# A four-stage residual vector quantizer on one core: the order of every engine's queue and the engines of its free steps are replaced

## The chip, the cores and the metric

The kernel runs on one core of one Trainium2 chip. Time is what the device takes for one execution, in microseconds. Beside the time of several runs there is one profiled execution, whose trace gives each instruction's start and end; its span runs from the first to the last instruction. The engines are TensorE (PE, matmuls), VectorE (DVE), ScalarE (ACT), GpSimd (POOL) and SyncE (SP, which here issues the large DMAs). Each engine works its own queue in the order in which the program put it there, and waits at an instruction until its inputs and buffers are ready.

## The reference

For two sequences of 16,000 rows of 512 values the kernel computes a three-tap filter along time, a SiLU, a four-stage residual quantization against codebooks of 8 entries each, and a second three-tap filter over the sum of the chosen entries.

```python
for i in range(K):                       # K = 3
    z = z + xp[:, i:i+T, :] * dw_enc[i][None, None, :]
z = _silu(z)
res = z
for s in range(Nq):                      # Nq = 4
    cb = codebooks[s]                    # 8 x 512
    d2 = (res . res)[..., None] - 2.0 * res . cb + (cb . cb)
    idx = d2.argmin(-1)
    sel = cb[idx]
    q = q + sel
    res = res - sel
for i in range(K):
    y = y + qp[:, i:i+T, :] * dw_dec[i][None, None, :]
```

## The kernel before

The rows are cut into 18 tiles, n = 0 to 17. A tile has G groups of 128 rows; G is 6 and 8 for the first two tiles, 16 for fourteen, 8 and 6 for the last two. The 512 channels lie in four blocks of 128 on the partitions. Each tile goes through these stages, whose names are the keys of the steps in the code (line numbers are those of the profile):

- load: SP issues one transposing DMA for each group (L599, L607, L613) into one of three buffers XT. The first two tiles come by plain DMAs and are turned on PE (pad, L580 and L590).
- taps, in two halves of two channel blocks: three scalings by a filter weight for each block (L640 on ACT, L641 on DVE, into TA and TB) and two additions on DVE (L393).
- exp (L646, ACT), plus1 (L647 on ACT or L648 on DVE), recip (L658, ACT) and gate (L393, DVE, ZB<-ZB,EX): the SiLU. exp and recip need different tables of ACT, so two or three halves go through exp, then the same ones through recip.
- score0: on PE the squared length of each row and its products with all 32 entries (L670, L677); DVE reads them out of PSUM (L711, L712).
- decide: the first three choices, a chain of small DVE operations, with a transpose and a correction on PE in between (L754, L764) and a small copy of the result by ACT or DVE (L758, L759). POOL copies one-hot rows (L746, L749).
- win0: the one-hot rows are turned on PE (L787) and copied (L792). resid: PE subtracts the three chosen entries from z in 4 units of two steps (L835, L840); the result is cast back into ZB by ACT (L862) or DVE (L863). The last two steps of a unit feed two casts.
- score3, decide3: the fourth choice in the same manner (L878, L879). win3: its one-hot rows are turned (L804) and copied (L810).
- back: the decoder filter as a matmul for each pair of groups (L912, L914, L916), cast into one of four buffers YB by ACT (L921) or DVE (L922), and stored by SP (L949).

The program is not written in its final order. The class Plan collects 2,404 steps, each with its engine, a cost for planning, and its dependencies. A step with the engine pair ACT and DVE is a free step: six kinds are free, the scalings of taps, plus1, the copies of pad, win0, win3 and of decide's transposed choice, the casts of resid and of back, and three small scalings of the setup. Two strings settle everything: RANK gives each step a number, and each engine's queue is sorted by it; WHERE gives one letter, A or D, for each free step in the order of the code.

```python
queue[s["on"]].append(s["n"])
for q in queue.values():
    q.sort(key=lambda n: -rank[n])
```

The loop in Plan.order then goes through the queues and hands out PSUM banks; where by its own costs PE would stand idle for over a microsecond it puts dummy matmuls ahead of the step (fill, L969). There are 413 of these in the kernel before. The dependencies, and with them every wait, come from the tiles that a step reads and writes.

Of the kernel before, what the change touches and what calls it, by code (L numbers as in the profile page):

```python
# [185 lines left out]
def kernel(  # L186
# [30 lines left out]
    NA = 4  # L217
    QUOTA = {"ACT": 4, "DVE": 4}
    DIGITS = "0123456789abcdefghijklmnopqrstuvwxyzABCDEFGHIJKLMNOPQRSTUVWXYZ"
    RANK = ("00010300000501090M0f0a0N080K0e010b030f0X0l0e0i0b0U0h0q0s000o000q0A0b0d0n0E040s0708020f0a0e060g0109040607090d0f0i0j02080a"  # L220
            "0c0e0g0h0m05050d070709020406040a0c0608010b0i0r03020A0H0K0v050c0T0V0Y1115191b0q0E0F0c0G0r0j0m0o1e1m1p1d1o1u0h0o0t1j1w1y0p"
            "0d0k0m030i0t0z0F0H0J0L0P0S0g0j0l0p0k0v0D0y0I0B0O0x0l130u0m0u0G0w0C0j1i0p1r0n1l0k1g0Q0h0g0R0W100Z120n1f171614181a1h1c1k0w"
            "0z0y1A0B1E0r0s1M1O1N1P1Q1R1S0k0t0L0u1T1V1X1Z1W1Y202122230l0v250w242628292a2b2c2d0n0x0P0y0z2i2j0A0B0T0R0C0D2n2m0E0F0U0V0G"
            "0H2t2A2D2H2J0K120N170P191m0M141t1s1n1q0x1t1x1v1z0D271B1C1D0C1F1G1H1I0J0O0h050b0708030i0g0a0604090c0f020j0l0d1L0I1J1K1U0M"
            "0N2e0Q2l0S2w0W2v0X2x0I0J2z2B2C2E2G2I2K0o0L130O2M2N2O2R2T2W2X2Y2Z300p0Q330R31343637383a3b3c0q0S3e0T0U3i3j0V0W3l1b0X0Y1d3n"
            "0Z101e3o11123t3w3x3z3B151l1c1t1f1u1p191n1a1o1f2h2k2f2g2o2p2q2r102L0t0o0B0u0k0m0e0q0A0n0z0r0p0v0x0s0y0w0Z2s0Y2u2y2F112P16"
            "182U152V2S3239353d1a3p1c3r1g3F1i3E13143D16173I3L3K3N3P3Q3S0r1d1p1g3U3W3Y403V3Z414243440s1i471j464a4c4b4d4e4f4g0u1k1v1l1m"
            "1x1y1n1o1z1A1p1q1D4u1r1s1C4x1v1w4H1x1z4Q4V4X4Z531L1P1S1Y2024211R1X1W221Y1Q1W1Y201Z1P1V1V2627181b3R1e1h3X48454k4l4p4s0t1t"
            "4z1u4v4w4y4A4C4D4E4F4G4I0v1y4L1A4J4K4M4P4R4S4U4W0w1D1J1F1G541M1I1J1O1N1K1M1S1R1N1O1U1T1T1Z5C21225F5H5J5L5O265W29282b2a2f"
            "2a292e2b2u2q2l2A2r2t2r2n2x2q2p0G0O0Q0E0D0T0M0I0N0C0R0F0K0J0P0H0S0L3k3g3h3f3m1f3q3s1k491h3v3u3y3A1j3C3H1q4m15110Y1a0Z0W17"  # L230
            "100V161912181c14130X0U3M3J3O1m3T1r1s4h1w4o1B4B1E4N1G4Y1B1C511E1H565a585c5e5h2Q5j0y1U5s1X5l5n5p5r5w5y5A5E5G5I0z235M245K5N"
            "5R5Q5T5Y60630C2d652f2g2e2d2h2i6e2f2l2m2i2h2n2o2j2k2t2v6C2u2z6L6N6P6T702I732S2G327D2K2L2C2M2E2C2N2D2R2F2F2U2H312O2N4n4i4q"
            "4j4r1F4t4O1K571h1i1b1v1u1s1g1d1r1x1w1o1n1l1e1q1k1j504T1I1H521L55591Q5o5d5f5g5b5i5m5k5q1Z5B215P255Z276425275V282c676b6a6d"
            "6f6h3G6j0D2p6r2s6m6o6q6s6u6v6w6x6y6z0E2w2o2y6A6D6F6E6G6H6I6J0F2B2s2D2F2w2x2G2H2z2v2J2K2A2B2V2Y2K7v33357J38397Q7S7W7Y813g"
            "2W3k303m312W3j2Z3w373b3n323l353d3o8j3q38342j2k6k2C2E6S6W6V7274767a0H2Q7f2T7c7e7g7i7j7k7m7o7q7s0I2Z2J307t7u7y7x7z7A7B7C0J"
            "347F36372P2Q3b3c2U2T3e3f2V2X3h3i2Y893p3r8h3t3v8n8p8r8t8A3G8I413u423w3z3N3l3U3o3r403t3P3v3v3O3m3Q3p3E1C1F1I1E1P1G1A1z1y1O"
            "1M1B1H1N1D1L1K1J5u5v5x5t5z235D5S2c6B625X615U6669686c2g6t1U1X251V1T1R292a1S26222820231Q241W0x0A6l6g6n6i6p2p2m6K2t6X2u752y"
            "772I7H2O2P7d2W2X7n7r7p7w7E7G7I0K3a2R3d7K7M7N7O7V7X7Z8486880L3s343u8b8f8i8l8o8q8s8u0M3x8x3y3z3a3c3C3D3h3d3E3H3i3f3J3K3j3k"
            "3T3V983W3Y9e9j9l9n9q453y4l3L4g3N3M4h3J4p3M3L4d3E4q3Q3Q4s3P4t3S3S6Q6O6M6R6U6Y6Z712M7L2n2d2c2i2e2j2k2l2h2w2m2g2b2q2o2r0B0G"
            "2s787b797h7l2L2N7P2S837R7T807U8285878a338w368y398G3b8H3A3B8F3F3I8K8O8N8Q8S8U8V0N3R8X3S8Y909295919497999a9b0O3X3r3Z9d9f9h"  # L240
            "9g9i9k9m9o0P439r46473z3A484a3C3F4b4c9F3D4e4f3G3H4i4j9R4m4na4a7a9abad4xak4B3U4C3V494A3T4F3X3Y4E3W4Gaz414W484R4c4g3L3M8R44"
            "499y9C9A9E9J9M9O0Q4k9U4o9Q9T9W9Z9Ya3a6aaacae0R4wag4zahajamanaparasau0U4Daw4H4I3Z404J4K41424L4M43464O4PaQ454S4Tb14X4Ybabd"
            "bgbjbn594h5c4k5f4n4E5e4p5n4u4z5g4o5r4A4H5k4r5o4t4B2L2A2I2G2J2E2z2M2y2x2v2D2R2B2Q2P2O2H8d8e8g8c8k8v8m8z3e8M8E8B8C8D8J3g8L"
            "8P3n9c30352Y36372U3a38323c33392S2V312Z2X2T938Z8W8T963s3q9p3x9x3B9H3I9V3Ka14r4uaf4v4yalaqaoataxaBaD0S4NaM4QaGaIaKaNaRaTaU"
            "aVaWaX0T4UaZ4VaYb0b2b3b4b5b6b70W4Z4a5152bi4d55564g4f585a4j4i5b5d4m4l5h5lbK5i5pbNbQbTbVbY5F4G5J4N5P4P4I5I4L5X4U4Q5O4O5S4R"
            "4N5Q4Q5T4T4R9u9s9t9v9w9B9z9D3Oai3l3s3f3h3t3i3g3w3k3u3p3n3o3q3m3e3x3j9L9I9G9K9N9P9S9X3Raya0a5a2a8av3YaAaC44aS47b849bb4bbo"
            "5054bl5357bpbsbrbvbybAbC0V5j4q5mbEbGbIbMbHbLbPbRbWbZ0X5u4x5wc1c3c5c6c7c8c9cb0Z5xcg5y5z4Bck5A5B4E4D5C5D4F4H5G5H4K4J5K5NcD"
            "5M5RcGcKcMcOcV5Zd1634X6f594Z6o5b6q5f506g586n5c516e576j5d525q5sbU5t5vc4cacccdcecfci0Y5E4I5LcmcqcscwcycAcCcEcJcL105WcP5YcN"
            "cRcUcTcWcXcYcZ12614W64654Z5066675251686955546c6d56ds6h6idF6m6pdNdUdWe0e56ye76G5s6S5y536O5v6UeT546M5u6Q5w566F5r6N5t553O3J"
            "3D3N3F3G3H3R3P3U3C3y3B3I3K3A3V3TaEaJaHaFaLaPaOb94ebtbfbebcbhbkbmbqbu4sc03Z4h404f4344424c3W4b4d4e484a4746453XbxbwbBbzbDbJ"  # L250
            "bFbO4vc24zcn4Ccp4McF5U5VcQ6062d3d6d5d9dbdedg136adj6bdidkdmdpdndqdtdvdxdy146kdC6ldzdAdHdGdKdMdPdS166sdV6u6v5h5k6w6x5ie86A"
            "6C5o5n6D6Eel5p6H6Jeu6L6PeFeIeKeMeO6VeW7e5K7m5Q577h5O7n5P587f5L7o5R597c5J7g5N5a4ybXbS4wchclcjco4Sd04o4w4y4x4n4q4r4v4A4u4s"
            "4p4t4l4j4k4m4icvcuctcrcxcBczcH4Ydfd2cS4VcId4d7d8da53dr5adQ5ee25ge66r6tdX6z6Beaefecehekemen176Ieq6KepeteweAevexeBeCeDeE18"
            "6ReG6TeHeJeLeNePeQeReS1b6XeU6Z70f0f67172f25C75765E5G777bfi5I7j7lfB7q7ufQfUfXfYg77Ggd7L5Z7Wgx5d7Kgj7Mgm5b7Q607U645c7S627X"
            "635e6W6YeV7374f3f5f4f7f8f9fb19795H7dfdfgfhfjfkflfmfnfofp1a7i5M7kfqfrfsfvfwfxfyfA1e7pfE7r7tfL5S7w7x5U5T7A7B5W5X7E7Fgc5Y7J"
            "7Ngk7T7ZgygCgGgHgI86gK8ggQ8i6e5h886a8bgN5f8e6c8f6d5g8m6g8n6h5i4K4O4L4J4G4C4D4P4M4FdldcdhdddodudwdB5mejdJdIdEdDdLdRdOdT5q"
            "ey5xeY5zeZ787afeftfufzfCfDe9fF1c7sfK7vfGfHfIfJfMfNfOfPfRfS1d7z5V7CfTfVfWfZg0g2g5g81i7Hgg7P7R61gu8081656682836867848769gL"
            "8h8lgSgTgUgVgW8qgY8v6l8x6m5k8s6j8u6k5j4T4V4S4Y4X4U4W1115e1dZdYe3e45l5jeb5Af1eeeiedegeoeresez5Bfa5Dfc5Fff7y7Dg1g4g3g6g9ga"
            "eXgb1f7Ige7Ogfghgignglgogpgqgrgs1g7Vgw7YgtgvgAgzgBgDgEgF1h85gJ898agM6b8c8dgPgO8j8kgR6f8o8pgX6i8r8tgZh0h1h2h38wh48yh58Ah6"
            "5m8z6n5l")  # L260
    WHERE = ("DADDADAADAADAADAADDDDDDDDDDAADADDAADDAAAAAADDDADDDDDDADDADADDAADADDDDDAADADAAAAADDDDDDDADADDAADADDDDDADAAAAAADADAAAAAAAA"
            "ADDADAAAAAAADAAAAAAAADDDDADDADDDADDDDDAAADDDDAADAAAAADADAAAAAADDDDADDDDAAADDDDDDDDDDAAAAAAAAADAAAAAAADADADAAAAAAADDAAAAA"
            "AAADDDDADDDDDDDDDDDDDAADAADAAAAAAAAAAAAAAAAADDDDDDDDDDDAADDDDDDDDDADAAAADAAADAAAAADAADDDAAAAAADAAAAAAAAAADDDDDDDDDDDADDD"
            "DDDAADDDADAAAAAAAAAAAAAAAADDDDDDDDDDDDDDDDDDADDAADADAAAAAADAAAAAAAAADAAAAAAAADDAAADAAAADDDDDDDDDDDDDDDDDDDDDDDDAAADAADAD"
            "AAAAAAAAADDADDDDDDDDDDDDADDDDDDDDDDAAADADADDDAAAAAADDAAAAADADDAADAAAADDDDDDDDDDDDDDDADADAAAAADDAAAADDDDAADDDDDDDDDDDDADD"
            "DADADDDA")
# [740 lines left out]
```

## Time and profile before

| | before |
|---|---|
| median of 3 runs | 602.56 us (601.38 to 603.75) |
| span of the profiled execution | 600.7 us |
| busy: PE, DVE, ACT, POOL | 500.1, 562.4, 548.7, 53.6 us |
| instructions on DVE and ACT | 1125 and 419 (26 of ACT's are table loads) |

The profiled execution has no time of its own beside its span; the median of the runs stands 1.9 us above that span. In the rows that follow, "busy" is the time in which at least one instruction of the group ran, "mean ns" is the duration of one, and what stands behind the second bar is the idle time of the engine just before instructions of the group and what ended it. A row of a timeline has the start, the duration, the engine, the line, the operation and its tiles.

### The profile page before, as it was taken

The page shows a single profiled execution, that of the slowest core. Times are in us where ns is not written, and L with a number is a line of the kernel's source. Part 1 is how long each engine was busy: PE and PEld are TensorE (multiplying, and loading weights), DVE is VectorE, ACT ScalarE, POOL GpSimd, SP SyncE. Part 2 cuts the span into 40 slices and gives each one's busy share as a digit, 9 for nine tenths or more (in the row PEclk, how much of TensorE's full clock was granted, in tenths as well). Part 3 has the DMA queues.
Part 4 walks back from the last instruction along what each step waited for, and adds up shares of the span by engine and source line. Part 5 has one row for each costly group of instructions (what it writes and reads, how often), then busy time and mean ns, then how long its engine had stood idle before and what let it go on. Part 6 is the DMA issues. An engine that isn't in the chain of part 4 may idle for free.

```text
span 600.7 us, 27780 instructions
## 1 busy us (share of the span) xinstructions
PE 500.1 (83%) x12632; PEld 241.1 (40%) x12632; DVE 562.4 (94%) x1125; ACT 548.7 (91%) x419; POOL 53.6 (9%) x86
## 2 busy tenths in 40 slices
...
DVE  7999999999999999999999999999999999996764
ACT  4889999999999999999999999999999999996454
...
GB/s 222 84 93 73 84 102 90 75 133 124 73 97 139 138 117 107 174 155 92 142 140 95 168 123 188 147 108 115 82 179 88 177 56 109 4 144 142 39 183 183
DMA packets 155564, 71.84 MB, mean 120 GB/s; under 512 B 146895, under 2 KB 146927, under 8 KB 155318
## 3 DMA queue, kind: packets, MB, share of 16 engines
...
## 4 chain that ended last, share of the span: by engine, by line
DVE 23%; PE 12%; SPq 8%; ACT 8%; issue 5%; DMA 1%; DVEq 0%; ACTq 0%
SPq L599 7%; DVE ZB L393 6%; DVE TB L641 3%; PE banks L835 3%; PE banks L912 3%; PE banks L677 2%; PE banks L840 2%; DVE TA L393 2%; ACT ZB L862 2%; DVE TA L641 2%; ACT EX L646 2%; DVE EX L648 1%; ACT YB L921 1%; DVE ZB L863 1%; DMA XT<-in_x_dram 1%
## 5 line engine op out<-in xcount | busy, mean ns | idle before, releaser
L921 ACT CAST YB<-banks 128x1024 bf16<-128x1024 f32 x115 | 111.6, 1037 | 12.9 <-PE banks L912 6.6
L646 ACT ACTIVATE EX<-ZB 128x4096 bf16<-128x4096 bf16 (+2 forms) x36 | 115.3, 3205 | 4.1 <-DVE ZB L393 3.9
L658 ACT ACTIVATE EX<-EX 128x4096 bf16<-128x4096 bf16 (+2 forms) x36 | 115.1, 3201 | 0.1
L862 ACT CAST ZB<-banks 128x1024 bf16<-128x1024 f32 (+2 forms) x109 | 97.7, 952 | 16.3 <-PE banks L840 16.3
L969 PE MATMUL banks<-MSK,IDENT 128*128 128x512 bf16 x413 | 103.5, 392 | 6.4 <-issue 2.6
L677 PE MATMUL banks<-ZB 128*32 128x64 bf16 x8064 | 90.4, 197 | 9.7 <-issue 6.0
L677 PEld LDWEIGHTS <-ZB 128*32 128x32 bf16 x8064 | 75.6, 95 | 52.6 <-issue 44.7
L912 PE MATMUL banks<-WDEC,OHW 128*128 128x512 bf16 x252 | 74.0, 382 | 14.3 <-ACT ZB L862 8.0
L840 PE MATMUL banks<-OHR,WR 32*128 32x512 bf16 (+2 forms) x1152 | 81.6, 355 | 0.1
L641 DVE TENSOR_SCALAR TB<-XT,WENC 128x2048 bf16<-128x2048 bf16 (+2 forms) x115 | 76.7, 676 | 1.6 <-issue 1.2
L393 DVE TENSOR_TENSOR ZB<-TA,TB 128x4096 bf16<-128x4096 bf16 (+2 forms) x36 | 73.0, 2028 | 0.8 <-ACT TB L640 0.4
L393 DVE TENSOR_TENSOR TA<-TA,TB 128x4096 bf16<-128x4096 bf16 (+2 forms) x36 | 72.7, 2020 | 0.5
L393 DVE TENSOR_TENSOR ZB<-ZB,EX 128x4096 bf16<-128x4096 bf16 (+2 forms) x36 | 72.3, 2017 | 0.3 <-ACT EX L658 0.2
L835 PE MATMUL banks<-ZB,IDENT 64*64 64x512 bf16 (+2 forms) x576 | 54.3, 368 | 13.4 <-DVE ZB L863 3.0
L749 POOL COPY OHD<-OHA 128x256 bf16<-128x256 bf16 (+2 forms) x36 | 27.5, 764 | 417.3 <-DVE OHA L393 417.3
L969 PEld LDWEIGHTS <-IDENT 128*128 128x128 bf16 x413 | 38.4, 100 | 49.7 <-issue 13.8
L640 ACT ACTIVATE TB<-XT,WENC 128x2048 bf16<-128x2048 bf16 (+2 forms) x29 | 53.2, 1845 | 3.6 <-DVE TA L393 2.0
L835 PE MATMUL banks<-ZB,UP 64*64 64x512 bf16 (+2 forms) x576 | 52.4, 353 | 0.0
L840 PEld LDWEIGHTS <-WR 32*128 32x128 bf16 x1152 | 23.4, 92 | 58.3 <-issue 50.1
L641 DVE TENSOR_SCALAR TA<-XT,WENC 128x2048 bf16<-128x2048 bf16 (+2 forms) x66 | 44.0, 676 | 1.5 <-DMA XT<-in_x_dram 1.4
L835 PE MATMUL banks<-ZB,DOWN 64*64 64x512 bf16 (+2 forms) x576 | 41.4, 363 | 0.0
L863 DVE CAST ZB<-banks 128x1024 bf16<-128x1024 f32 (+2 forms) x35 | 32.8, 950 | 7.3 <-PE banks L840 7.3
...
## 6 DMA issues: line engine op xcount, KB each, us to landing
...
out_dram<-YB SPq DMA_DIRECT2D x31, 2.0 KB
...
```

Source lines behind the costliest of these rows:

```text
L393: add("DVE", cost, key, lambda: nc.vector.tensor_tensor(out=out, in0=a, in1=b, op=op), reads, writes, **kw)
L640: either({"ACT": act(R), "DVE": dve(R, 3.84) + 0.06}, key, lambda dst=dst, src=src, w=w: nc.scalar.mul(dst, src, w), lambda dst=dst, src=s ...
L641: lambda dst=dst, src=src, w=w: nc.vector.tensor_scalar(out=dst, in0=src, scalar1=w, scalar2=None, op0=ALU.mult),
L646: add("ACT", act(2 * R), ("exp", n, h), lambda: nc.scalar.activation(v(ex), Z, ACT.Exp, scale=-1.0), zt, [("EX", sl), "ACTTAB"], hold="E")
L658: nc.scalar.add_instruction(mybir.InstActivation(name=nc.get_next_instruction_name(), engine=mybir.EngineType.Activation, func=ACT.Reciprocal,
L677: nc.tensor.matmul(o[HB * q:HB * (q + 1), u * ZW:(u + 1) * ZW].rearrange("p (s c) -> p s c", s=2), lhsT=blk, rhs=both, start=False, stop=( ...
L835: nc.tensor.matmul(at(r)[to], lhsT=dia[h, h], rhs=Z[h, i, r:G:RG, :], start=start, stop=False)
L840: nc.tensor.matmul(at(r), lhsT=WR[v][g, i * P:(i + 1) * P], rhs=W[g, v // 3, 0:rows_of[r], :], start=False, stop=stop)
L862: either({"ACT": act_psum(2 * k * P), "DVE": dve(2 * k * P)}, key(1), lambda dst=dst, src=src: nc.scalar.copy(dst, src()), lambda dst=dst, ...
L912: nc.tensor.matmul(o, lhsT=W[:, k, PADC:PADC + P], rhs=WDEC[u], start=True, stop=not wrap)
L921: either({"ACT": act_psum(1024), "DVE": dve(1024)}, key, lambda dst=dst, box=box: nc.scalar.copy(dst, ps(box)), lambda dst=dst, box=box: n ...
L969: nc.tensor.matmul(PS[j // 2][:, 512 * (j % 2):512 * (j % 2) + NMK * ZW], lhsT=IDENT, rhs=MSK.rearrange("p u w -> p (u w)"), start=True, s ...
```

## The change

Only the two strings are replaced, RANK (4,808 characters, two for each step) and WHERE. Every step and its function stay.

```diff
-    RANK = ("00010300000501090M0f0a0N080K0e010b030f0X0l0e0i0b0U0h0q0s000o000q0A0b0d0n0E040s0708020f0a0e060g0109040607090d0f0i0j02080a"
+    RANK = ("00010200000a0905090b070G060F0c010408080f0h0a0g0g100d0i0m000v080g0E00020c260n2D0k1J04270p0z014h0703010306070c0g0h0j02050b"
...
-    WHERE = ("DADDADAADAADAADAADDDDDDDDDDAADADDAADDAAAAAADDDADDDDDDADDADADDAADADDDDDAADADAAAAADDDDDDDADADDAADADDDDDADAAAAAADADAAAAAAAA"
+    WHERE = ("AADDAAAADAAAAADDADDDDDDDDDDDADADDAAAAADAAAADDDDDDADAAADDADADADDDDDDDAAADAAAAAAAADDDDDDDDAADDAADDADDDDAAADAAADADAAAAAAAAA"
...
```

What it makes of the queues, read from the built programs. Free steps that change their engine, as net counts (a 2048 is a tile 128x2048, and so on):

| | DVE | ACT |
|---|---|---|
| taps, 2048 into TB (L641, L640) | 88 to 99 | 24 to 13 |
| taps, 2048 into TA | 51 to 49 | 5 to 7 |
| taps, 1024 into TA; 768 into TA; 768 into TB | 8 to 7; 7 to 6; 13 to 15 | 0 to 1; 1 to 2; 3 to 1 |
| resid casts, 1024 (L863, L862) | 19 to 13 | 93 to 99 |
| resid casts, 512; 256 | 13 to 8; 3 to 4 | 11 to 16; 5 to 4 |
| win3 copies, 1024; 384 (L810) | 9 to 5; 1 to 0 | 5 to 9; 1 to 2 |
| pad copies, 1024 (L590) | 5 to 3 | 2 to 4 |
| back casts (L922, L921) | 11 to 10 | 115 to 116 |
| win0 copies, 1024 (L792) | 9 to 10 | 5 to 4 |
| plus1, 2048; 1536 (L648, L647) | 3 to 2; 3 to 4 | 1 to 2; 1 to 0 |
| setup scaling WR | 1 to 0 | 2 to 3 |
| all instructions but table loads | 1125 to 1116 | 393 to 402 |

ACT still changes its table 26 times, in the same groups of two and three halves. The dummy matmuls go from 413 to 423; ahead of the first score0 there are 20 instead of 39, and a new group of 3 stands before the last step of PE.

The order near the end, for tiles 14 to 17. In PE's queue, a number behind a star is a count of steps:

```diff
-resid14*4 score015*2 resid14*3 score016 decide15 score016 resid14 back13 decide15 back13*4 decide15 score314 decide15 score314 back13*3 win015 score314 resid15 decide16 resid15 score314 decide16 resid15*2 score017 decide16 resid15*2 decide16 score017 resid15*2 win314 win016
+resid14*4 score015*2 resid14*3 score016 resid14 decide15 back13 decide15 score016 back13*3 score314 decide15 back13 decide15 back13 score314 back13 win015 score314 back13 resid15*2 decide16 score314 resid15 decide16 resid15*3 decide16 resid15 score017 decide16 score017 resid15 win016 win314
```

On DVE the two gates of tile 17 were instructions 999 and 1003 of 1125, ahead of most of decide15; they become 1041 and 1042 of 1116, behind decide15, most of decide16 and the first cast of resid15. On ACT the two recips of tile 17 were 347 and 349 of 393 and become 364 and 367 of 402, behind six and seven casts of back13. In SP's queue loads and stores of the same tiles are interleaved otherwise: from tile 9 on, the longest run of loads between two stores was 18 (the last of load14 and all 17 of load15, ahead of the first store of tile 9) and is 16 (load12, ahead of the first store of tile 6). In the setup some steps of tables that are not needed at once move behind the first taps, gates and decide steps.

More of the change, by code (lines that the diff above doesn't have):

```diff
@@ L219 @@
     DIGITS = "0123456789abcdefghijklmnopqrstuvwxyzABCDEFGHIJKLMNOPQRSTUVWXYZ"
-    RANK = ("00010300000501090M0f0a0N080K0e010b030f0X0l0e0i0b0U0h0q0s000o000q0A0b0d0n0E040s0708020f0a0e060g0109040607090d0f0i0j02080a"
[L221 to L260, printed above, removed]
```

50 lines of the change are left out of this document (45 added, 5 removed).

## The prediction

> **What bounds the kernel now.** I read the page's sums and slices first, then the busy time of each engine by stretches of the span.
>
> ```profile
> PE 500.1 (83%) x12632; PEld 241.1 (40%) x12632; DVE 562.4 (94%) x1125; ACT 548.7 (91%) x419; POOL 53.6 (9%) x86
> DVE  7999999999999999999999999999999999996764
> ACT  4889999999999999999999999999999999996454
> ```
>
> ```profile
> core 0: us, PE busy (x) PEld busy (x) DVE busy (x) ACT busy (x) POOL busy (x), PEclk, DMA share, GB/s
> 0.00:60.00 60.00, 44.04 (x549) 22.55 (x549) 53.91 (x153) 47.06 (x61) 4.77 (x29) 0.91 0.51 118
> 60.00:523.91 463.91, 386.29 (x10146) 184.76 (x10142) 456.17 (x827) 453.22 (x306) 45.36 (x47) 0.99 0.61 117
> 523.91:537.75 13.84, 13.46 (x415) 5.78 (x407) 12.86 (x26) 13.68 (x12) 0.97 (x1) 1.00 0.45 155
> 537.75:552.71 14.96, 14.53 (x390) 7.20 (x382) 11.38 (x43) 9.69 (x11) 1.14 (x4) 1.00 0.31 109
> 552.71:594.55 41.84, 41.78 (x1157) 20.85 (x1153) 26.76 (x79) 24.41 (x31) 1.37 (x6) 1.00 0.37 128
> 594.55:600.70 6.15, 0.00 (x1) 0.00 (x0) 1.33 (x2) 0.66 (x1) 0.00 (x0) 0.77 0.62 202
> ```
>
> From 60 to 524 us DVE is busy for 456.17 of 463.91 us and ACT for 453.22: two engines at 98%, and neither can give the other work without becoming the bound. From 524 to 594.55 DVE and ACT thin out and PE is full (13.46 + 14.53 + 41.78 of 70.64 us). So there are two regimes. The front runs at the pace of DVE and ACT together; the tail, from the first resid step of tile 14 on, is PE's remaining queue without a hole, then the last casts and stores. Its landmarks:
>
> ```profile
> 523.23 0.68 DVE L792 COPY OHR<-banks 128x1024 bf16<-128x1024 bf16 x1
> 523.71 0.41 PE L835 MATMUL banks<-ZB,IDENT 64*64 64x512 bf16 x4
> 536.80 0.95 DVE L393 TENSOR_TENSOR ZB<-ZB,EX 128x1536 bf16<-128x1536 bf16 x1
> 552.71 0.34 PE L670 MATMUL banks<-MSK,IDENT 128*128 128x384 bf16 x1
> 593.96 0.59 PE L912 MATMUL banks<-WDEC,OHW 128*128 128x512 bf16 x2
> ```
>
> The first row is win0 of tile 14, the second the start of its resid, the third the last gate (tile 17), the fourth the start of score0 of tile 17, the fifth PE's last matmuls. The last gate is ready at 537.75 and PE takes it up only at 552.71: 15 us of slack. What shortens the kernel is an earlier arrival at resid14, as long as that slack isn't used up.
>
> **What the moved steps cost.** The dependent work stays; the free steps change sides. Prices, from the groups with shapes kept apart:
>
> ```profile
> L641 DVE TENSOR_SCALAR TB<-XT,WENC 128x2048 bf16<-128x2048 bf16 x88 | 65.1, 747 | 1.5 <-issue 1.2
> L641 DVE TENSOR_SCALAR TA<-XT,WENC 128x2048 bf16<-128x2048 bf16 x51 | 37.5, 744 | 1.5 <-DMA XT<-in_x_dram 1.4
> L863 DVE CAST ZB<-banks 128x1024 bf16<-128x1024 f32 x19 | 23.1, 1216 | 2.6 <-PE banks L840 2.6
> L863 DVE CAST ZB<-banks 128x512 bf16<-128x512 f32 x13 | 8.7, 684 | 4.5 <-PE banks L840 4.5
> L810 DVE COPY OHW<-banks 128x1024 bf16<-128x1024 bf16 x9 | 6.1, 680 | 0.1
> L922 DVE CAST YB<-banks 128x1024 bf16<-128x1024 f32 x11 | 13.3, 1219 | 2.0 <-PE banks L912 1.7 <-PE banks L914 0.3
> ```
>
> ```profile
> L640 ACT ACTIVATE TB<-XT,WENC 128x2048 bf16<-128x2048 bf16 x24 | 48.0, 2014 | 3.4 <-DVE TA L393 2.0 <-DMA XT<-in_x_dram 1.4
> L640 ACT ACTIVATE TA<-XT,WENC 128x2048 bf16<-128x2048 bf16 x5 | 10.0, 2003 | 0.3 <-DVE OHA L741 0.3
> L862 ACT CAST ZB<-banks 128x1024 bf16<-128x1024 f32 x93 | 89.9, 1027 | 12.4 <-PE banks L840 12.4
> L862 ACT CAST ZB<-banks 128x512 bf16<-128x512 f32 x11 | 6.0, 584 | 2.9 <-PE banks L840 2.9
> L810 ACT COPY OHW<-banks 128x1024 bf16<-128x1024 bf16 x5 | 5.3, 1061 | 0.0
> L921 ACT CAST YB<-banks 128x1024 bf16<-128x1024 f32 x115 | 111.6, 1037 | 12.9 <-PE banks L912 6.6 <-PE banks L916 3.3 <-DVE ZB L863 2.1
> ```
>
> A scaling costs ACT 2.01 us and DVE 0.75, a ratio of 2.7; a cast out of f32 PSUM costs ACT 1.03 and DVE 1.22. The change sends scalings to DVE and casts to ACT, each to the side where it is comparatively cheap:
>
> - The 2048 scalings: DVE 11 x 0.747 - 2 x 0.744 = +6.7; ACT -11 x 2.014 + 2 x 2.003 = -18.1.
> - The resid casts: DVE -6 x 1.216 - 5 x 0.684 = -10.7; ACT +6 x 1.027 + 5 x 0.584 = +9.1.
> - The win3 copies and one back cast: DVE -4 x 0.680 - 1.219 = -3.9; ACT +4 x 1.061 + 1.037 = +5.3.
> - All other moves of the table are single or paired and small. By the rows of their shapes they come to -1.2 on DVE and +2.3 on ACT.
>
> Sums: DVE -9.1, ACT -1.4. Durations overstate, since an instruction starts a little before the one ahead ends:
>
> ```profile
> 593.51 2.37 DVE L922 CAST YB<-banks 128x1024 bf16<-128x1024 f32 x2 [0.92 <-PE banks L912]
> 539.30 2.92 ACT L921 CAST YB<-banks 128x1024 bf16<-128x1024 f32 x3
> ```
>
> Two casts of 1.22 take 2.37 (0.07 less), three of 1.04 take 2.92 (0.09 less for each further one). With 9 instructions fewer on DVE and 9 more on ACT the busy times should be some -8.5 and -2.3: DVE about 554, ACT about 546.5.
>
> **Where that lands.** What counts is the work queued ahead of resid14. Counting the free steps ahead of the copy at 523.23 in DVE's queue, priced from start to start: 9 resid casts fewer (-8.2), 2 back casts (-2.3), 2 pad copies (-1.2) and a plus1 (-0.7) fewer, 3 scalings more net (+2.9), the rest -0.4: -9.9 us. It is more than DVE's whole saving because 6 scalings of tile 17 now come later. On ACT, ahead of the last cast of back12, which ended 0.7 us behind that copy: 11 scalings fewer (-18.7), 9 resid casts (+6.7), 2 pad copies and 2 back casts (+3.7) more, the rest +1.8: -6.5 us. Whether the front gains by the one or the other depends on who waits for whom at the gate:
>
> ```profile
> L393 DVE TENSOR_TENSOR ZB<-ZB,EX 128x4096 bf16<-128x4096 bf16 x28 | 63.8, 2284 | 0.2 <-ACT EX L658 0.2
> ```
>
> ```profile
> 440.52 3.63 ACT L658 ACTIVATE EX<-EX 128x4096 bf16<-128x4096 bf16 x1
> 445.90 2.28 DVE L393 TENSOR_TENSOR ZB<-ZB,EX 128x4096 bf16<-128x4096 bf16 x1
> ```
>
> Now DVE hardly waits there (0.2 us in 28). But it isn't far behind: here, for the second half of tile 13, the recip ends at 444.15 and the gate starts at 445.90, a slack of 1.75 us, and by such pairs 29 of the 36 halves have under 3 us. When DVE's queue gets 9.9 us shorter and ACT's 6.5, DVE reaches the gates up to 3.4 us earlier against ACT, so part of the lead turns into waits. The bounds are -6.5 (ACT paces) and -9.9 (DVE paces); I take -7.0, near ACT's, as each half must pass through ACT twice.
>
> The tail: PE's work from resid14 on is the same list in another order, and 3 dummy matmuls more, ahead of its last step. Their price:
>
> ```profile
> L969 PE MATMUL banks<-MSK,IDENT 128*128 128x512 bf16 x413 | 103.5, 392 | 6.4 <-issue 2.6 <-DVE RC L727 1.7 <-DVE ZB L863 0.9
> ```
>
> 103.5 / 413 = 0.25 us each: +0.7. The other 7 of the ten more stand where PE has room (386.29 of 463.91) and cost nothing; were PE full there, 1.8 us.
>
> Tile 17's front is what now comes late. Its gates have 4.3 us more work ahead on DVE, its recips 5.6 more on ACT. With unchanged idle time the last gate ends not at 537.75 but near 542 to 543.4. Three more steps of resid15 stand ahead of score0 of tile 17 on PE; a short and a long one run densely in
>
> ```profile
> 550.08:552.71 2.63, 2.63 (x43) 0.89 (x40) 2.46 (x11) 0.35 (x1) 0.15 (x1) 1.00 1.02 391
> ```
>
> (40 of the 43 matmuls are theirs), and the third, of 8 matmuls, is about 0.5: 3.1 us. PE gets there at 552.71 - 7.0 + 3.1 = 548.8. So 5.4 us of the 15 remain, and the delay is covered. Without that cover each microsecond would lengthen the kernel by one.
>
> SP: reordered loads and stores cost nothing as long as a store isn't late for the buffer's next use.
>
> ```profile
> SPq L599 7%; DVE ZB L393 6%; DVE TB L641 3%; PE banks L835 3%; PE banks L912 3%; PE banks L677 2%; PE banks L840 2%; DVE TA L393 2%; ACT ZB L862 2%; DVE TA L641 2%; ACT EX L646 2%; DVE EX L648 1%; ACT YB L921 1%; DVE ZB L863 1%; DMA XT<-in_
> 281.30 1.26 SPq L599
> ```
>
> In the chain of waits a load's issue takes 1.26 us, so a store behind 16 loads is up to 20 us late, where 18 made it 23; a YB buffer is written again one tile later, some 33 us (463.91 us for about 14 tiles). Loads of tiles 8 and 9 are on the chain now (7%), and the front asks for them some microseconds earlier; bounds 0 and +2, taken as 0, because 18 issues (23 us) and a few stores fit into a tile's 33. POOL is at 9% and DVE's and ACT's setup steps only change places: 0.
>
> **The sum.** 600.7 - 7.0 + 0.7 = 594.4 for the span, and 1.9 more for the median: 596.3, rounded to 596. By the bounds: 593.4 with -9.9, and 600 where half the gain goes into new waits.
>
> The Trainium skill has a sentence that speaks against the change: "TensorE: Matmul & The Clock Gate", section "Architectural detail", says that ScalarE's and VectorE's queues are strictly first in, first out. No row here tests it against a case where an engine could have passed a stalled instruction; by it every wrong guess of a duration in the new order holds up all that is queued behind, which is the third rival.
>
> **The rivals.**
>
> 1. DVE paces (15%). ACT has idle time of its own in the front (12.9 of the first 60 us, 10.7 in 60 to 524) and recovers part of its lag. Then -9.9 + 0.7: 591.5 span, 593.4 median. For it: ACT's largest waits are for PE's banks (12.4 on L862, 12.9 on L921), which come earlier when DVE is earlier. Against it: two passes through ACT for every half.
> 2. The gain goes into the wait for tile 17 (17%). PE comes early to resid14 but the late gate holds it at score017. From that point 41.84 - 3.1 + 0.7 = 39.4 us of PE work and 6.15 of last casts and stores remain, so a span of 600.7 needs the gate at 555.2, 12 us behind what its queues say. For it: gate17 now stands behind the first cast of resid15, which hangs on the chain of decide15. Against it: 12 us is as much as DVE's whole idle time until 524 (523.91 - 510.08 = 13.8). At that point the median is 602.6, no change.
> 3. Slower by stalled queue heads (13%). The place is DVE's queue at the gates: the slack ahead of most gates is under 3 us already, and where ACT's recip comes late by one long instruction the whole queue stands. The price is one exposed reciprocal:
>
> ```profile
> L658 ACT ACTIVATE EX<-EX 128x4096 bf16<-128x4096 bf16 x28 | 101.6, 3630 | 0.1
> ```
>
> 3.6 us. The gain is gone at 2 of 28 halves exposed (6.3 / 3.6), 3 make it slower beyond the noise, 4 give 600.7 + 4 x 3.6 - 6.3 = 608.8 span, 610.7 median. Against it: the present order, under the same tight load, loses 0.2 us at these gates.
>
> A new hole in PE's tail would have a second price in the page named above, section "Part 1: The HAM clock gate": an idle window of about 3.4 us halves the clock until the next busy one. The tail shows a clock of 1.00 throughout and no such hole, the first 60 us show 0.91. By an estimate from the page's figures that would add some 1.7 us to the second rival.
>
> **How the numbers follow.** My forecast, ACT's pace with a covered tail, has 55%, its own range 593 to 600. Measured runs of this kernel tell about 0.5% (3.0 us) from no change: faster means under 599.5, slower over 605.6. The forecast and rival 1 give 70% faster; rival 2 is no change (17%); rival 3 is slower (13%). Leaving a tenth out on each side: 589 (DVE's pace and some idle time recovered) to 605 (two to three halves exposed).
>
> **What would show it.** Right: DVE busy near 554 and ACT near 546.5; the copy of win0 of tile 14 near 517; some 5 us between the last gate and the first score0 matmul of tile 17; PE full from there on; DVE's idle time ahead of gates up to a few microseconds. Wrong: idle time of DVE between 60 and 510 us well over the present 8 (waits for EX or ZB), PE idle ahead of L670 of tile 17, or SP's stores waiting long in the middle.

## The result, and the profile after

The changed kernel takes 598.27 us (median of 9 runs, 596.61 to 602.07) where the kernel before takes 601.88 (9 runs in the same series). The ratio is 0.9947, with a 95% interval of 0.9924 to 0.9971: faster by 0.53%, about half of what was forecast (596, or 1.1% below 602.56). The span of its profiled execution is 597.8 us against 600.7. Every run's time is about 2 us above its span; the spans of the nine runs lie between 594.7 and 600.3, so that a number read from one profiled execution can be off from the typical one by up to 3 us.

The page of the changed kernel, its sums and the slices of DVE and ACT:

```profile
PE 508.9 (85%) x12642; PEld 243.0 (41%) x12642; DVE 548.6 (92%) x1116; ACT 546.4 (91%) x428; POOL 72.2 (12%) x86
DVE  6999999799999989999989989996999999987754
ACT  5899999799999989999979999997899999998654
```

DVE's busy time fell by 13.8 us and ACT's by 2.3 (forecast 8.5 and 2.3), so the work was saved. For DVE not all of it is work: its instructions' durations, added up, fell from 634.6 to 624.6 us, by 10.0, and the rest is that successive instructions overlap for longer in the new order. But the slices now have 7s and 8s in the middle, where there were only 9s. Busy time by stretch, cut at three of the events of before (start of resid of tile 14, end of the last gate, PE's last matmul):

```profile
core 0: us, PE busy (x) PEld busy (x) DVE busy (x) ACT busy (x) POOL busy (x), PEclk, DMA share, GB/s
60.00:520.34 460.34, 390.23 (x10083) 184.25 (x10083) 440.84 (x816) 441.05 (x308) 63.27 (x47) 0.97 0.59 117
520.34:551.67 31.33, 31.25 (x843) 13.73 (x846) 27.28 (x76) 27.90 (x28) 1.90 (x6) 1.00 0.39 137
551.67:591.47 39.80, 38.93 (x1115) 20.05 (x1115) 24.51 (x74) 25.56 (x33) 0.94 (x4) 1.00 0.36 124
591.47:597.80 6.33, 0.00 (x0) 0.00 (x0) 1.23 (x1) 0.28 (x1) 0.00 (x0) 0.88 0.59 184
```

The tail is as long as it was: from resid14 to the last matmul 71.1 us (591.47 - 520.34) against 70.8, and PE is busy for 70.2 of them. So the gain of the kernel is the gain of the front: resid14 starts at 520.34 instead of 523.71, 3.4 us earlier where 7.0 was forecast. In the front DVE now idles for 19.5 of 460.34 us (7.7 of 463.91 before). DVE's waits of the changed kernel, total, times and longest:

```profile
DVE TA L641 <- DMA XT<-in_x_dram: 8.0, 4, 4.5
DVE RC L727 <- PE banks L764: 4.4, 2, 2.5
DVE TA L641 <- issue: 2.4, 1, 2.4
DVE ZB L393 <- ACT EX L658: 1.1, 1, 1.1
```

The first row was 1.4 us before. Its two large cases, and the one that the profile puts down to "issue", in the timeline of DVE; the number in brackets is the idle time before the instruction:

```profile
210.38 0.75 DVE L641 TENSOR_SCALAR TA<-XT,WENC 128x2048 bf16<-128x2048 bf16 x1 [2.39 <-issue]
...
311.53 0.75 DVE L641 TENSOR_SCALAR TA<-XT,WENC 128x2048 bf16<-128x2048 bf16 x1 [2.94 <-DMA XT<-in_x_dram]
...
410.37 0.75 DVE L641 TENSOR_SCALAR TA<-XT,WENC 128x2048 bf16<-128x2048 bf16 x1 [4.52 <-DMA XT<-in_x_dram]
```

They are the first scalings of tiles 8, 11 and 14. The loads are late, and SP's queue says why. The transposing loads of the kernel before and then of the changed one, from tile 7 to tile 14: count, shortest, median and longest issue in ns, and first and last start.

```profile
L599 SPq DMA_TRANSPOSE XT<-in_x_dram x128: 1188/1267/2392, 151.5 to 408.6; - x128
```

```profile
L599 SPq DMA_TRANSPOSE XT<-in_x_dram x128: 1189/1267/2726, 147.0 to 405.1; - x128
L949 SPq DMA_DIRECT2D out_dram<-YB x55: 227/440/1815, 179.9 to 394.8; - x55
```

The stream of loads of eight tiles takes 257 to 258 us in both kernels, however much work DVE and ACT have left. In the changed kernel there are 142 issues in it (128 of L599 and 14 at the tiles' edges). Some run much longer than the median, so that they take 1.48 us each on average, 210.5 us in all. The 55 stores among them come to 32.0 us and the small steps between them to 9.9. So SP is at work for 252.4 of 259.4 us. It was as full in the kernel before, with 253.2 of 259.0. SP's longest waits of the changed kernel from 148 to 406 us:

```profile
SPq L599 <- ACT TB L640: 6.6, 1, 6.6
SPq L949 <- ACT YB L921: 5.0, 2, 3.3
SPq L949 <- ACT OT L758: 1.5, 1, 1.5
```

The first is the wait that ends as the stream starts, at 147.0: a load stands until ACT has done with its buffer XT. The other two are stores that wait for their cast, with the loads queued behind them. They make up most of the 7.0 us in which SP stands still after that; no later load of the stretch waits for its buffer for more than 0.3 us.

The front's gain of 3.4 us is close to the 4.5 us by which the stream started earlier (147.0 against 151.5). Up to there SP still waited for the engines, and their saving showed; from there on it did not.

### The profile page after: what moved, and what is told of

The parts are those of the page before. It is cut to its first block, busy times and chain, and to the rows that moved or that the text cites. A ratio compares the mean times of both kernels' runs of the same rounds, so it can differ in the third digit from the quotient of the medians.

```text
span 597.8 us, 27797 instructions
## 1 busy us (share of the span) xinstructions
PE 508.9 (85%) x12642; PEld 243.0 (41%) x12642; DVE 548.6 (92%) x1116; ACT 546.4 (91%) x428; POOL 72.2 (12%) x86
## 5 line engine op out<-in xcount | busy, mean ns | idle before, releaser
L921 ACT CAST YB<-banks 128x1024 bf16<-128x1024 f32 x116 | 113.6, 1034 | 12.5 <-PE banks L912 10.0
L862 ACT CAST ZB<-banks 128x1024 bf16<-128x1024 f32 (+2 forms) x119 | 105.7, 952 | 14.2 <-PE banks L840 13.5
L969 PE MATMUL banks<-MSK,IDENT 128*128 128x512 bf16 x423 | 105.9, 393 | 5.0 <-issue 4.4
L912 PE MATMUL banks<-WDEC,OHW 128*128 128x512 bf16 x252 | 77.1, 390 | 16.4 <-ACT ZB L862 8.5
L749 POOL COPY OHD<-OHA 128x256 bf16<-128x256 bf16 (+2 forms) x36 | 44.3, 1230 | 385.9 <-DVE OHA L393 367.3
L641 DVE TENSOR_SCALAR TB<-XT,WENC 128x2048 bf16<-128x2048 bf16 (+2 forms) x128 | 84.9, 677 | 0.1
L969 PEld LDWEIGHTS <-IDENT 128*128 128x128 bf16 x423 | 40.2, 101 | 51.6 <-issue 13.2
L641 DVE TENSOR_SCALAR TA<-XT,WENC 128x2048 bf16<-128x2048 bf16 (+2 forms) x62 | 42.2, 684 | 11.0 <-DMA XT<-in_x_dram 8.0
L835 PEld LDWEIGHTS <-IDENT 64*64 64x64 bf16 x576 | 20.8, 104 | 40.4 <-issue 33.3
L648 DVE TENSOR_SCALAR EX<-EX 128x4096 bf16<-128x4096 bf16 (+2 forms) x33 | 36.8, 1114 | 0.4 <-ACT EX L646 0.4
```

Source lines behind the costliest of these rows:

```text
L641: lambda dst=dst, src=src, w=w: nc.vector.tensor_scalar(out=dst, in0=src, scalar1=w, scalar2=None, op0=ALU.mult),
L749: add("POOL", 1.5, key(4.2), lambda s=s, OH=OH: nc.gpsimd.tensor_copy(OHD[b][:, 0, 0:G, 2 * s:2 * s + 2, :], two(OH)), [("OHA", n % NOH)], ...
L835: nc.tensor.matmul(at(r)[to], lhsT=dia[h, h], rhs=Z[h, i, r:G:RG, :], start=start, stop=False)
L862: either({"ACT": act_psum(2 * k * P), "DVE": dve(2 * k * P)}, key(1), lambda dst=dst, src=src: nc.scalar.copy(dst, src()), lambda dst=dst, ...
L912: nc.tensor.matmul(o, lhsT=W[:, k, PADC:PADC + P], rhs=WDEC[u], start=True, stop=not wrap)
L921: either({"ACT": act_psum(1024), "DVE": dve(1024)}, key, lambda dst=dst, box=box: nc.scalar.copy(dst, ps(box)), lambda dst=dst, box=box: n ...
```

## The experiments

Theory A: SP's queue, loads and stores together, paces the stretch up to 410 us, and the work saved on DVE and ACT became waits for XT. Theory B: DVE and ACT pace, and the rest of the gain was lost in stalls inside the new order. The ratios below are against the kernel before on the same chip; the changed kernel has 0.9947.

**Engines alone, order alone.** RANK was written anew so that a step's number is its place in the sequence in which one kernel's plan issued the steps. This leaves that kernel's queues as they are, and any choice of engines can be put into them.

```diff
 # e1
-    RANK, WHERE of the kernel before
+    RANK = places in the sequence of the kernel before;  WHERE of the changed kernel
 # e2
+    RANK = places in the sequence of the changed kernel; WHERE of the kernel before
```

> The new choice of engines (WHERE) in the old order. Theory A (SP's stream of loads paces 60 to 410 us, so DVE and ACT work saved there turns into waits for XT): DVE busy near 549 and ACT near 546 as in the changed kernel, but the time hardly moves, 599 to 602 us. Theory B (DVE and ACT pace, and the gain was lost in stalls that the new order brought): the old order has few stalls, so the saving shows in full, 594 to 597 us.

> The new order with the old choice of engines. Theory A: the stream of loads starts some 4 us earlier, as in the changed kernel (first load of tile 4 issued near 55 instead of 59 us), and that is the gain: 598 to 601 us in spite of DVE busy near 557 to 562. Theory B: no work is saved and the new stalls stay: 602 to 606 us.

Measured: 639.2 us, ratio 1.058 [1.053, 1.063], and 654.7 us, ratio 1.083 [1.078, 1.087]. Both theories missed by 30 us and more. DVE's busy time in e2 is as expected (560.7 us); in e1 it is 557.1 instead of 549, with the same instructions as in the changed kernel. In the stretch from 60 to 410 us (first e1, then e2)

```profile
60.00:410.00 350.00, 290.45 (x7062) 136.57 (x7055) 328.88 (x576) 324.31 (x218) 26.90 (x33) 0.95 0.58 117
```

```profile
60.00:410.00 350.00, 292.16 (x6771) 135.85 (x6770) 310.91 (x546) 313.65 (x206) 37.70 (x32) 0.98 0.54 109
```

DVE idles for 21 and 39 us and ACT for 26 and 36 (6.6 and 8.2 in the kernel before, by its row below). In e1 the longest sum is ACT's casts waiting for PE:

```profile
ACT ZB L862 <- PE banks L840: 31.8, 27, 5.1
```

Here each order fits only its own choice of engines: the two strings WHERE differ in 123 of their 608 letters, many more than the net counts of the table, and to change them with the order left in place, or the other way about, costs ten times the gain and more. These two runs don't decide between A and B.

**The stores of tiles 2 to 13 taken out**, in both kernels (those rows of the output stay unwritten):

```diff
-        for p0, p1, lo, hi in parts:
+        for p0, p1, lo, hi in (() if 2 <= st["n"] <= 13 else parts):
```

> The changed kernel without the stores of tiles 2 to 13 (their rows of the output are not written). Theory A: 37 us of issue time leave SP between 60 and 410 us, the loads come early, DVE's three waits for XT of 2 to 4.5 us (9.9 us in all) fall under 2 us, and the time falls by 4 to 8 us, to 590 to 594. Theory B: waits for XT are not what paces, the time stays within 2 us of the changed kernel, 596 to 598.

> The kernel before without the stores of tiles 2 to 13. Theory A: its waits for XT are small (1.4 us on DVE), DVE and ACT pace it as much as SP does, so it gains less than the changed kernel from the same cut: 599 to 601 us. Theory B: no change, 601 to 602.

Measured: the changed kernel 588.0 us, ratio 0.9737 [0.9701, 0.9772], which is 2.1% below the changed kernel with its stores; the kernel before 600.6 us, 0.9954 [0.9928, 0.9979]. The same cut gives the one some 12.6 us and the other 2.8. Theory A's order of the two holds and theory B falls; A had put the changed kernel's gain too low (590 to 594 us). The stretch from 60 to 410 us in four kernels, one row each: before, changed, before without stores, changed without stores.

```profile
60.00:410.00 350.00, 286.99 (x7345) 136.94 (x7341) 343.38 (x594) 341.82 (x222) 30.84 (x33) 0.99 0.65 123
```

```profile
60.00:410.00 350.00, 295.37 (x7351) 138.13 (x7350) 332.64 (x593) 333.44 (x227) 52.21 (x34) 0.98 0.63 121
```

```profile
60.00:410.00 350.00, 290.58 (x7360) 137.16 (x7361) 345.24 (x600) 343.55 (x224) 32.34 (x33) 0.98 0.49 82
```

```profile
60.00:410.00 350.00, 300.81 (x7502) 140.41 (x7497) 342.31 (x607) 341.87 (x235) 53.46 (x35) 0.98 0.50 84
```

Third number after the window: DVE's busy time. Its idle time is 6.6, 17.4, 4.8 and 7.7 us. Only the changed kernel has some ten microseconds to give back, and it does when SP is free. Without stores resid14 starts at 510.53 us, and in the kernel before without stores at 521.37: 10.8 us of front are saved, a little more than the forecast's DVE bound of 9.9. By the medians, the change is worth 13.1 us without stores (0.9954 - 0.9737 of 602) and 3.2 with them.

**The stores moved, not removed.** Taking them out frees SP's queue and also the DMA engines. To tell these apart, POOL issues the stores, each behind its last cast, first all of them and then those of tiles 0 to 13 (SP has no loads left for the others); the same in the kernel before. RANK is written anew as above, so that the loads keep their order.

```diff
-            add("SP", 0.55 * len(parts), ("back", ...
+            add("POOL" if n < 14 else "SP", 0.55 * len(parts), ("back", ...
...
-            nc.sync.dma_start(out=view[p0:p1, lo:hi, :], ...
+            (nc.gpsimd if st["n"] < 14 else nc.sync).dma_start(out=view[p0:p1, lo:hi, :], ...
```

> The changed kernel with all stores issued by POOL's queue, each right behind its last cast in POOL's order; all bytes are still moved. Theory A, in the form that SP's issue time paces: the loads come as early as without stores and the time falls toward 588 to 593 us, less what POOL's one-hot copies lose behind the stores. If the bytes of the stores on the DMA engines are what slows the loads, the waits for XT stay and the time stays at 595 to 599. Theory B: 597 or more.

> The changed kernel with the stores of tiles 0 to 13 issued by POOL and those of tiles 14 to 17 by SP, which has no loads left then. Theory A: the front runs as with all stores on POOL (resid of tile 14 starts near 512.5 us), and the slow end goes (from PE's last matmul to the end of the span 6.3 us as in the changed kernel instead of 9.0): span near 590.5, time 591 to 596. Theory B: no better than the changed kernel, 597 or more.

> The kernel before with the stores of tiles 0 to 13 issued by POOL. Theory A: DVE and ACT pace it even with a free SP (without stores at all it gained 2.8 us), so this gives 0 to -3 us, 599 to 602, against -6 in the changed kernel. If it falls as far as the changed kernel did, to 596 or less, the move of the stores is worth the same in both, and the new order and engines have nothing to do with it.

Measured: all stores on POOL 598.9 us, ratio 0.9925 [0.9898, 0.9951]; tiles 0 to 13 on POOL 593.7 us, 0.9850 [0.9820, 0.9879]; the kernel before with the same 604.7 us, 1.0039 [1.0007, 1.0072]. With all stores on POOL, the stretch from 60 to 410 us is

```profile
60.00:410.00 350.00, 291.03 (x7368) 139.44 (x7428) 340.65 (x602) 339.95 (x235) 90.36 (x101) 0.99 0.69 125
```

DVE's idle time is down to 9.4 us with all bytes still moving (125 GB/s against 121). The time of 598.9 us lies where the traffic was expected to put it (595 to 599), so the waits have to decide. DVE's idle time ahead of its scalings of XT into TA, in the changed kernel, with all stores on POOL, and with those of tiles 0 to 13:

```profile
L641 DVE TENSOR_SCALAR TA<-XT,WENC 128x2048 bf16<-128x2048 bf16 (+2 forms) x62 | 42.2, 684 | 11.0 <-DMA XT<-in_x_dram 8.0
```

```profile
L641 DVE TENSOR_SCALAR TA<-XT,WENC 128x2048 bf16<-128x2048 bf16 (+2 forms) x62 | 42.4, 687 | 2.7 <-DMA XT<-in_x_dram 1.3
```

```profile
L641 DVE TENSOR_SCALAR TA<-XT,WENC 128x2048 bf16<-128x2048 bf16 (+2 forms) x62 | 42.8, 693 | 3.2 <-issue 1.8
```

The waits go though the traffic stays, so it is SP's queue that held the loads up: the time of the stores' issues and the waits for casts ahead of them, which these runs don't tell apart. With all stores on POOL this doesn't show in the time. The end is longer, 9.0 us from PE's last matmul where it was 6.3; and the profiled execution is the fastest of its seven runs (595.1 us), so its rows show this kernel at its best. With SP issuing the last stores the time is 593.7 us, which beats both others. There the profiled execution is the slowest of its six (596.3 us). The forecast of 591 to 596 held; the path that it gave (resid14 at 512.5, an end of 6.3 us) isn't seen in this execution: resid14 starts at 516.2, DVE idles for 12.4 us, and the end takes 7.3 us.

In the kernel before the move gives nothing, it even costs 0.4%. So the gain of 1.5% belongs to the move and the new order together. To move the stores is worth 1.0% in the changed kernel, to leave them out 2.1%; where the other 1.1% goes wasn't settled.

**Extra work on DVE.** Where SP paces, extra work must be swallowed. The first attempt did a scaling of X twice:

```diff
-        tt(Z, v(ta), v(tb), ALU.add, ...
+        add("DVE", ..., lambda: (nc.vector.tensor_scalar(out=tb[:, 1], in0=X[:, 2*h+1, 2:2+G, :], scalar1=WENC[...]) if 4 <= n <= 13 else None, nc.vector.tensor_tensor(out=Z, in0=v(ta), in1=v(tb), op=ALU.add)), ...
```

> The changed kernel with one 2048 scaling on DVE done twice in each half of tiles 4 to 13: 20 x 0.66 = 13 us of extra DVE work, the result is the same. Theory A: DVE waits some 10 us for XT in this stretch, so much of it is absorbed: +3 to +6 us, 601 to 604. Theory B: DVE paces, nearly all shows: +10 to +13, 608 to 611.

> The same 13 us of extra DVE work in the kernel before. It waits for XT for only 1.4 us on DVE and 1.4 on ACT. Both theories: +9 to +13 us, 611 to 615; theory A needs this to be clearly more than what the same work adds to the changed kernel.

Measured: 620.9 us, 1.0305 [1.028, 1.033], and 639.2 us, 1.0597 [1.057, 1.062]. They don't measure what they were meant to. The second scaling stands, in the order of the program, behind loads that already overwrite X for a later tile, so it reads that tile's data and waits for it:

```profile
DVE TB L645 <- DMA XT<-in_x_dram: 17.2, 6, 4.2
```

They are left out of the argument. The second attempt works in place and touches no load (in0=tb[:, 1], times 1.0):

> The changed kernel with an extra DVE pass over TB (2048 a partition, times 1.0, in place) ahead of the sum in each half of tiles 4 to 13: 20 x 0.66 = 13 us, no new reads of XT. Theory A: DVE is idle for 17.4 us between 60 and 410 us here and for 7.7 without stores, so some 9.7 us are absorbed: +3 to +6, 601 to 604. Theory B: +10 to +13, 608 to 611.

> The same in the kernel before. DVE is idle for 6.6 us between 60 and 410 us, and for 4.8 without stores, so 2 us can be absorbed: +9 to +13 us by both theories, 611 to 615; theory A needs a clearly larger rise than in the changed kernel.

Measured: the changed kernel 603.6 us, 1.0029 [1.0007, 1.0052], so 4.9 us more than without the extra work (1.0029 - 0.9947 of 602); the kernel before 613.5 us, 1.0194 [1.0171, 1.0217], 11.7 us more. The same 13 us cost the kernel before nearly their full price and the changed kernel little more than a third. Theory A's numbers held in both, and theory B's 608 to 611 us for the changed kernel did not. The row of the changed kernel with the extra work shows where it went:

```profile
60.00:410.00 350.00, 293.07 (x7277) 136.44 (x7260) 344.06 (x612) 331.67 (x224) 43.33 (x34) 0.97 0.61 120
```

DVE's idle time there is 5.9 us instead of 17.4.

**The dummy matmuls ahead of decide.** DVE's two waits for RC stand behind such groups. Near 114 us, on PE:

```profile
108.84 4.33 PE L969 MATMUL banks<-MSK,IDENT 128*128 128x512 bf16 x13 [2.38 <-issue]
113.01 0.22 PE L754 MATMUL banks<-IDENT,OHA 128*128 128x128 bf16 x1
```

```diff
-            if s["fill"]:
+            if s["fill"] and not (s["k"][0] == "decide" and s["k"][1] >= 2):
```

> The changed kernel without the dummy matmuls ahead of decide steps from tile 2 on (they add nothing to the result). DVE's two waits for the correction matmuls (RC from banks, 2.5 and 1.9 us near 114 and 347 us) stand behind such a group. Theory A: the loads pace, so taking these waits away gives at most 1 us: 597 to 599. Theory B: the waits are part of what was lost, 3 to 4 us come back: 594 to 595.

Measured: 607.3 us, ratio 1.0087 [1.0059, 1.0116], 1.4% slower than the changed kernel. Both theories missed. DVE's waits for RC (4.4 us in the changed kernel) are gone, but DVE waits more for PE elsewhere (rr from banks 11 us in all instead of 3), and its waits for XT stay (6.5 us from 60 to 410 us). PE's mean granted clock is 0.953 to 0.965 in these runs and 0.964 to 0.981 in those of the changed kernel. That lower clock alone doesn't explain the loss: the changed kernel's run at 0.964 took 598.27 us, its median. The cause stays open.

## Why the prediction was right, and where its size was off

- **That two engines at 98% would pass a cut of their work on: right in direction.** The prices of the moved steps were right: durations fell by 10.0 us on DVE where 9.1 were added up, by 1.7 on ACT where 1.4 were, and ACT's busy time is right to the tenth. DVE's busy time fell by 3.8 us more than its durations, by overlap, for which the sum has no term.
- **The term that was mis-sized is SP's.** The prediction set it to 0 with bounds of 0 and +2, because 18 issues of 1.26 us and a few stores fit into a tile's 33 us. Each part of that was too favourable: 17.75 issues take 1.48 us on average and not 1.26, there are 7 stores at 0.58, and 1.2 us of small steps go between them. That makes 26.3 + 4.0 + 1.2 = 31.5 us of the 32.4 that a tile takes in this stretch, and most of the remaining 0.9 is waits ahead of stores. SP had no room, and the 7% on SP's loads in the chain of waits pointed at it. The term measured +10.8 - 3.4 = 7.4 us: without stores the front gains 10.8, with them 3.4. By the medians it is 13.1 - 3.2 = 9.9.
- **That ACT paces the front (-7.0) and not DVE (-9.9): wrong.** With SP out of the way the front gains 10.8 us, DVE's bound and a little more. The wait at the gates that was to eat the difference is 1.1 us in all.
- **That 596 came so near is in part luck.** The front was to gain 7.0 us and gained 3.4. Taking ACT's pace instead of DVE's made the forecast gain 3.8 us too small (7.0 against 10.8), and setting SP's term to nothing made it 7.4 us too large; the two errors partly cancel.
- **That the tail stays covered: right in its effect, wrong in its number.** The last gate ends at 551.67 and not near 543. The work that DVE does up to its end is the same in both kernels, 522.9 us of busy time; but DVE idles for 28.8 us up to there instead of 14.8, and 11.8 of these 14 us more arise in the front. The forecast had left the idle time unchanged. PE takes the gate's product up at 552.13, after 0.46 us instead of 5.4, but PE is full up to there (31.25 of 31.33 us). Rival 2 named this place; it cost nothing.
- **The dummy matmuls: right.** Three ahead of PE's last step cost 0.64 us, from 590.01 to 590.65; the tail is 0.3 us longer.
- **Rival 3, stalled heads at the gates: it didn't happen** (1.1 us). The stalls came at the loads, a place that no rival named. One sign of being wrong did show: DVE's idle time from 60 to 510 us is 19.4 us, well over the 8 named, though the largest part of it is waits for XT and not for EX or ZB.

The Trainium skill, "DMA: Bandwidth & Descriptors", section "Issuing engines are not separate DMA queues", says that issuing from several engines saves only the sequencer's time, which is usually small beside the DMA itself. The first half agrees with these runs: POOL's stores freed SP's queue and left the traffic as it was. The second does not hold here: a load takes SP 1.48 us on average and lands a median of 3.3 us after its issue (with the stores of tiles 0 to 13 on POOL), the issues fill SP's queue, and freeing it of 37 us between 60 and 410 us was worth about 1% of the kernel.
